# Squared-ReLU attention and a mixture-of-depths FFN on one core: score and index operations moved to VectorE, the sigmoid issued later, a load split around the FFN weights

## The chip, the core and the metric

The kernel runs on one core of a Trainium2 chip. The metric is the time of one execution in microseconds on the device; lower is better. In the text PE is TensorE, DVE is VectorE, ACT is ScalarE and POOL is GpSimd. Each engine executes its own queue of instructions in order and waits at an instruction until its inputs and its output buffer are ready.

## What is computed

For 8 batches of 12 heads, 448 tokens and 64 elements per head, attention without a softmax, and on its result, seen as 448 rows of 768, a feed-forward layer (FFN) for the 128 rows of each batch with the highest score:

```python
scores = scale * np.matmul(q, k.transpose(0, 1, 3, 2))
attn = np.maximum(scores, 0.0) ** 2 / S
x = np.matmul(attn, v)                  # then heads side by side: (8, 448, 768)
...
scores = np.einsum('bsd,d->bs', x, w_gate)
out = x.copy()
for b in range(B):
    top_idx = np.argpartition(-scores[b], capacity)[:capacity]
    xe = x[b, top_idx]
    h = np.maximum(xe @ w1, 0.0)
    ye = h @ w2
    g = 1.0 / (1.0 + np.exp(-scores[b, top_idx]))
    out[b, top_idx] = x[b, top_idx] + g[:, None] * ye
```

The FFN is 768 to 1024 to 768, and the inputs are float32; the kernel works in bfloat16.

## The kernel before

**Attention in pairs.** The work is cut into 48 steps t, one for each pair of heads, six to a batch (L356). `transposes(t)` (L152) turns q and k of a pair with PE and copies them out of PSUM on DVE (qkt, L170). `scores(t, c)` (L173) computes one of four chunks of keys; `relu_square` (L187) applies Relu on ACT (r_sb, L192) and squares on DVE (a_sb, L193); `attend` (L196) multiplies by v and, after the last chunk, ACT copies the result to xT (L210). Step t issues the scores of chunks 0 and 1, the attend of chunks 2 and 3 of step t-1, the transposes of step t+1, then the scores of chunks 2 and 3 and the attend of chunks 0 and 1.

**The MoE of a batch** is the generator `moe(b)` (L216). It becomes active when the batch's attention is done, and `advance` (L341) issues a piece of it twice in each step of the next batch, by a credit in microseconds; the `yield` numbers are the pieces' prices. So the MoE of batch b runs among the six pairs of batch b+1, and that of batch 7 by itself at the end. It computes the scores of all tokens (sc_ps, L221), copies them (bc, L224), transposes x chunk by chunk into x_sb (L230, L233), turns the scores into columns (cols, L242), splits each score into three bfloat16 parts that are written to columns 2 to 4 of tok (L245 to L250; columns 0 and 1 hold the row number as two integers), counts each token's rank on DVE with a tie-break table (L257), and makes from the rank a one-hot matrix (hot, L273). A matmul of hot and tok gives the row number and score of each of the 128 chosen tokens (sel_ps, L280), and DVE copies it (sel, L283). From sel come the row index idx (L286, L287), the score g (L289, L290) and its sigmoid on ACT (L291). hot also gathers the rows (xe_ps, L300); two layers follow (h_ps, L311; ye_ps, L323); ACT scales by g (gye, L327), and an indirect DMA adds the result to the output rows (L330), which were stored before by L269.

**Queues.** Every DMA is issued by POOL, in program order: `load(b, h0, h1)` (L96) makes nine DMAs, one for q, four for k and four for v. In order POOL issues the load of batch 0 in three parts with the identity matrix between, the gate weights, w1 and w2 (L117, L118), the load of batch 1 (L119), three kinds of tables by iota (slot_i L128, tie_i L134, tok_i L141 and L142), and then what belongs to the steps: the load of batch b+2 at the first step of batch b (L370), and the POOL work of moe. DVE turns the tables into slot_row (L130), tie (L136) and tok (L146); these are ahead of the loop in the program, and the framework chooses where they stand in DVE's queue. Inside the loop the order of the instructions on each engine is that of the program. There are three buffers each of q, k and v, and two of x_sb and of tok.

Of the kernel before, what the change touches and what calls it, by code (L numbers as in the profile page):

```python
# [8 lines left out]
FP32 = mybir.dt.float32  # L9
# [3 lines left out]
AF = mybir.ActivationFunctionType  # L13
ALU = mybir.AluOpType
# [6 lines left out]
def kernel(  # L21
# [11 lines left out]
    nc = tc.nc  # L33

    B, H, S, Dh = q.shape
    HD = H * Dh
    F = moe_w1.shape[1]
    CAP = int(moe_capacity)
    P = 112
    NC = S // P  # L40
# [14 lines left out]
    small = ctx.enter_context(tc.tile_pool(name="small", bufs=2))  # L55
# [23 lines left out]
    def load_q(b, h0, h1):  # L79
        nc.gpsimd.dma_start(  # L80
            out=q_sb[b % NBUF][:, h0:h1],
            in_=q[b, h0:h1].rearrange("h (p c) d -> p h c d", c=NC))

    def load_kv(t_sb, src, b, h0, h1):
        t = t_sb[b % NBUF]
        for par in range(2):
            hs = slice(h0 + par, h1, 2)
            lo, hi = (4, 3) if par == 0 else (3, 4)
            nc.gpsimd.dma_start(  # L89
                out=t[0:64, hs, 0:lo, :],  # L90
                in_=src[b, hs, 0:64 * lo].rearrange("h (p c) d -> p h c d", c=lo))
            nc.gpsimd.dma_start(  # L92
                out=t[64:128, hs, 0:hi, :],
                in_=src[b, hs, 64 * lo:S].rearrange("h (p c) d -> p h c d", c=hi))

    def load(b, h0, h1):  # L96
        load_q(b, h0, h1)
        load_kv(k_sb, k, b, h0, h1)
        load_kv(v_sb, v, b, h0, h1)
# [10 lines left out]
    for i in range(1, NBUF):  # L110
        zero_halves(i)

    wg_cols = const.tile([128, NM], BF16)
    nc.gpsimd.dma_start(out=wg_cols, in_=moe_w_gate.rearrange("(m p) -> p m", p=128))
    w1_sb = const.tile([128, NM, F], BF16)
    w2_sb = const.tile([128, NF, HD], BF16)
    nc.gpsimd.dma_start(out=w1_sb, in_=moe_w1.rearrange("(m p) f -> p m f", p=128))  # L117
    nc.gpsimd.dma_start(out=w2_sb, in_=moe_w2.rearrange("(m p) f -> p m f", p=128))  # L118
    load(1, 0, H)  # L119

    wg_rep = const.tile([128, NM, 128], BF16)
    nc.vector.tensor_copy(out=wg_rep,
                          in_=wg_cols.unsqueeze(2).to_broadcast([128, NM, 128]))
# [13 lines left out]
                            op0=ALU.is_gt, op1=ALU.mult)  # L137
# [78 lines left out]
    def moe(b):  # L216
# [21 lines left out]
        for c in range(NC):  # L238
            nc.tensor.matmul(out=col_ps[:, c:c + 1], lhsT=bc[0:1, c * P:(c + 1) * P],
                             rhs=one_f, is_transpose=True, start=(c == 0), stop=(c == NC - 1))  # L240
        cols = small.tile([P, NC], FP32, name="cols")
        nc.vector.tensor_copy(out=cols, in_=col_ps)  # L242
        tk = tok[b % 2]
        rem = small.tile([P, NC, 2], FP32, name="rem")
        nc.gpsimd.tensor_copy(out=tk[:, :, 2], in_=cols)  # L245
        nc.gpsimd.tensor_tensor(out=rem[:, :, 0], in0=cols, in1=tk[:, :, 2], op=ALU.subtract)
        nc.gpsimd.tensor_copy(out=tk[:, :, 3], in_=rem[:, :, 0])
        nc.gpsimd.tensor_tensor(out=rem[:, :, 1], in0=rem[:, :, 0], in1=tk[:, :, 3],
                                op=ALU.subtract)
        nc.gpsimd.tensor_copy(out=tk[:, :, 4], in_=rem[:, :, 1])  # L250
        yield 0.3

        rank = small.tile([P, NC], FP32, name="rank")
# [2 lines left out]
        def rank_chunk(c):  # L256
# [17 lines left out]
            out=hot, in0=slot_row.unsqueeze(1).to_broadcast([P, NC, CAP]),  # L274
            in1=rank.unsqueeze(2).to_broadcast([P, NC, CAP]), op=ALU.is_equal)
# [6 lines left out]
        sel = small.tile([CAP, 5], FP32, name="sel")  # L282
        nc.vector.tensor_copy(out=sel, in_=sel_ps)  # L283
        idx = small.tile([CAP, 1], INT32, name="idx")
        row = small.tile([CAP, 1], FP32, name="row")
        nc.gpsimd.tensor_tensor(out=row, in0=sel[:, 0:1], in1=sel[:, 1:2], op=ALU.add)  # L286
        nc.gpsimd.tensor_copy(out=idx, in_=row)  # L287
        g = small.tile([CAP, 1], FP32, name="g")
        nc.gpsimd.tensor_tensor(out=g, in0=sel[:, 4:5], in1=sel[:, 3:4], op=ALU.add)  # L289
        nc.gpsimd.tensor_tensor(out=g, in0=g, in1=sel[:, 2:3], op=ALU.add)  # L290
        nc.scalar.activation(out=g, in_=g, func=AF.Sigmoid)  # L291
        yield 0.2

        xeT = moe_pool.tile([128, NM, CAP], BF16, name="xeT")
# [11 lines left out]
        for half in range(2):  # L306
# [8 lines left out]
            nc.scalar.activation(out=hT[:, half * 4:half * 4 + 4, :], in_=ps, func=AF.Relu)  # L315
            yield 0.67

        gye = moe_pool.tile([CAP, HD], FP32, name="gye")
        for half in range(2):
            cols_d = slice(half * 384, half * 384 + 384)  # L320
# [10 lines left out]
            out=out.rearrange("b s d -> (b s) d"),  # L331
            out_offset=bass.IndirectOffsetOnAxis(ap=idx[:, :1], axis=0),
            in_=gye, in_offset=None, element_offset=b * S * HD, compute_op=ALU.add)
# [19 lines left out]
    with tc_manual:  # L353
        transposes(0)
        share = MOE_US / (2 * NHP) * 1.05
        for t in range(NT + 1):  # L356
            b, hp = divmod(t, NHP)
            if t < NT:
                scores(t, 0)
                scores(t, 1)  # L360
                relu_square(t, 0)
                relu_square(t, 1)
            if t > 0:
                attend(t - 1, 2)
                attend(t - 1, 3)
                if t % NHP == 0:
                    active.append(moe(t // NHP - 1))
            if t < NT:
                if hp == 0 and b + 2 < B:
                    load(b + 2, 0, H)  # L370
                if t + 1 < NT:
                    transposes(t + 1)
                advance(share)
                scores(t, 2)
                scores(t, 3)
                relu_square(t, 2)
                relu_square(t, 3)
                attend(t, 0)
                attend(t, 1)
                advance(share)  # L380
        while active:
            advance(10.0)
# [35 lines left out]
```

## Time and profile before

| | us |
|---|---|
| median of 3 runs | 312.34 |
| lowest and highest run | 312.20, 314.26 |
| the profiled execution | 315.93 |
| its span, first to last instruction | 314.2 |
| PE busy | 238.0 (76%) |
| ACT busy | 196.6 (63%) |
| DVE busy | 176.6 (56%) |
| POOL busy | 103.8 (33%) |

The rows further down come from one profiled execution. Times in them are microseconds from the start of its span. A line of a timeline names the start, the duration, the engine, the line of the kernel, the operation, the tile written and the tiles read, shapes, how many instructions are merged, and in brackets how long the engine stood idle before and what ended that wait. A digit of the busy tenths covers 1/40 of the span, 7.9 us.

### The profile page before, as it was taken

The numbers are of one execution on the slowest core, as the hardware profiler recorded it, in microseconds if no ns is written. First come the engines' busy times: TensorE is split into PE (matmuls) and PEld (weight loads), VectorE is DVE, ScalarE is ACT, GpSimd is POOL, SyncE is SP. The second block draws the span as 40 slices with busy tenths as digits, with TensorE's granted clock in tenths as the row PEclk, the third lists the DMA queues.
The fourth block names the chain that finished last, engine by engine and source line by source line (L and its number), as shares of the span: only waits on it lengthen the run. The fifth ranks groups of instructions, "written<-read, shape, count | busy, mean of one in ns | idle before, by whom it ended". The sixth has DMA issues, their size and how long they took to land.

```text
span 314.2 us, 6208 instructions
## 1 busy us (share of the span) xinstructions
PE 238.0 (76%) x2496; PEld 134.4 (43%) x2496; DVE 176.6 (56%) x378; ACT 196.6 (63%) x306; POOL 103.8 (33%) x191
## 2 busy tenths in 40 slices
PE   2597029649985899759984999499979998799480
PEld 1143014426452554436443554255445545455460
DVE  4378006934668165954577466936595568664500
ACT  1399006646974489728882799459875887496120
POOL 8991065730091204550085007420221023102301
PEclk9999756968997799979999899979995999799785
DMA  3999999993079801990099505990214012401603
GB/s 42 112 156 211 206 193 172 192 224 129 2 92 180 218 2 15 173 272 34 2 120 189 184 0 70 184 241 0 32 22 176 2 7 46 175 2 11 217 0 50
DMA packets 41580, 34.21 MB, mean 109 GB/s; under 512 B 14800, under 2 KB 38864, under 8 KB 40656
## 3 DMA queue, kind: packets, MB, share of 16 engines
q0 software_dynamic: 41552, 33.83, 64.2%
q8 instruction: 19, 0.31, 0.4%
q14 instruction: 9, 0.07, 0.1%
HBM read 39.32 MB, written 14.16 MB: 170 GB/s over the span
## 4 chain that ended last, share of the span: by engine, by line
PE 28%; issue 24%; DMA 24%; POOL 11%; DVE 6%; ACT 4%; POOLq 1%; ACTq 0%; DVEq 0%
DMA q_sb<-in_q_dram 13%; DMA k_sb<-in_k_dram 7%; PE o_ps L204 7%; PE s_ps L180 5%; PE h_ps L311 4%; PE ye_ps L323 4%; DMA out_dram<-x_sb 3%; ACT r_sb L192 3%; DVE trash L257 2%; PE xe_ps L300 2%; POOL v_sb L92 2%; PE s_ps L184 2%; DVE x_sb L233 2%; POOL tok L245 2%; POOL k_sb L89 1%
## 5 line engine op out<-in xcount | busy, mean ns | idle before, releaser
L192 ACT ACTIVATE r_sb<-s_ps 128x896 bf16<-128x896 f32 x192 | 148.2, 829 | 50.7 <-PE s_ps L180 49.5
L193 DVE TENSOR_TENSOR a_sb<-r_sb 128x896 bf16<-128x896 bf16 x192 | 103.6, 563 | 86.6 <-ACT r_sb L192 86.2
L204 PE MATMUL o_ps<-a_sb,v_sb 128*64 128x448 bf16 x384 | 61.6, 397 | 2.0 <-DVE a_sb L193 1.7
L330 POOL DMA_INDIRECT out_dram<-gye,idx x8 | 13.4, 1674 | 130.7 <-ACT gye L327 130.7
L180 PE MATMUL s_ps<-qkt 64*128 64x448 bf16 x288 | 50.0, 383 | 2.2 <-ACT r_sb L192 1.0
L170 DVE COPY qkt<-t_ps 128x960 bf16<-128x960 bf16 x48 | 31.2, 650 | 20.2 <-PE t_ps L165 20.2
L159 PE MATMUL t_ps<-ident,q_sb 112*64 112x112 bf16 x384 | 19.4, 224 | 20.0 <-DMA q_sb<-in_q_dram 14.5
L204 PEld LDWEIGHTS <-v_sb 128*64 128x64 bf16 x384 | 18.6, 112 | 32.1 <-issue 26.3
L311 PE MATMUL h_ps<-xeT,w_sb 128*128 128x128 bf16 x384 | 28.1, 227 | 1.3 <-ACT xeT L302 1.3
L159 PEld LDWEIGHTS <-q_sb 112*64 112x64 bf16 x384 | 17.6, 118 | 26.3 <-DMA q_sb<-in_q_dram 20.1
L92 POOL DMA_DIRECT2D v_sb<-in_v_dram x20 | 16.5, 824 | 36.8 <-DMA q_sb<-in_q_dram 21.3
L210 ACT ACTIVATE xT_sb<-o_ps 128x448 bf16<-128x448 f32 x48 | 26.6, 554 | 0.0
L311 PEld LDWEIGHTS <-w_sb 128*128 128x128 bf16 x384 | 23.6, 102 | 5.5 <-issue 4.3
L291 ACT ACTIVATE g<-g 128x1 f32<-128x1 f32 x8 | 1.6, 203 | 38.6 <-POOL g L290 38.6
L323 PE MATMUL ye_ps<-w_sb,hT 128*128 128x384 bf16 x128 | 24.9, 328 | 0.0
L180 PEld LDWEIGHTS <-qkt 64*128 64x128 bf16 x288 | 12.8, 95 | 28.4 <-issue 20.4
L165 PE MATMUL t_ps<-ident,k_sb 128*64 128x128 bf16 x384 | 21.4, 229 | 3.8 <-DMA k_sb<-in_k_dram 3.8
L230 PE MATMUL x_ps<-ident,xT_sb 128*112 128x128 bf16 x192 | 15.8, 223 | 10.0 <-DVE x_sb L233 8.0
L257 DVE SCALAR_TENSOR_TENSOR trash<-bc,cols,tie 112x448 bf16<-112x448 f32 x32 | 21.6, 675 | 0.2
L89 POOL DMA_DIRECT2D v_sb<-in_v_dram x20 | 19.1, 958 | 7.0 <-DMA w_sb<-in_moe_w_dram 6.8
L280 PE MATMUL sel_ps<-tok,hot 112*128 112x5 bf16 x32 | 2.0, 168 | 25.5 <-POOL tok L250 18.5
L300 PE MATMUL xe_ps<-hot,x_sb 112*128 112x128 bf16 x192 | 20.1, 284 | 0.0
(57 smaller groups left out, 250.4 us busy)
## 6 DMA issues: line engine op xcount, KB each, us to landing
out_dram<-x_sb POOLq DMA_DIRECT2D x8, 1344.0 KB, 6.2
q_sb<-in_q_dram POOLq DMA_DIRECT2D x7, 672.0 KB, 10.1
w_sb<-in_moe_w_dram POOLq DMA_DIRECT2D x2, 1536.0 KB, 16.0
k_sb<-in_k_dram POOLq DMA_DIRECT2D x14, 192.0 KB, 10.3
v_sb<-in_v_dram POOLq DMA_DIRECT2D x14, 192.0 KB, 8.0
k_sb<-in_k_dram POOLq DMA_DIRECT2D x14, 144.0 KB, 10.2
v_sb<-in_v_dram POOLq DMA_DIRECT2D x14, 144.0 KB, 11.0
q_sb<-in_q_dram POOLq DMA_DIRECT2D x1, 336.0 KB, 5.1
```

Source lines behind the costliest of these rows:

```text
L92: nc.gpsimd.dma_start(out=t[64:128, hs, 0:hi, :], in_=src[b, hs, 64 * lo:S].rearrange("h (p c) d -> p h c d", c=hi))
L159: nc.tensor.matmul(out=ps[64 * hh:64 * hh + 64, c * P:(c + 1) * P], lhsT=qs[:, h0 + hh, c, :], rhs=ident[:P, :P], is_transpose=True, start ...
L170: nc.vector.tensor_copy(out=sb, in_=ps)
L180: nc.tensor.matmul(out=ps[:, hh, :S], lhsT=sb[rows, S + c * 128:S + (c + 1) * 128], rhs=sb[rows, :S], start=True, stop=True)
L192: nc.scalar.activation(out=r[:, :n], in_=ps[:, :n, :S], func=AF.Relu)
L193: nc.vector.tensor_tensor(out=a[:, :n], in0=r[:, :n], in1=r[:, :n], op=ALU.mult)
L204: nc.tensor.matmul(out=o_ps[t][rows, :], lhsT=vs[:, 2 * hp + hh, c, :], rhs=a[:, hh if c < 3 else 0, :], start=(c == 0), stop=(c == 3), sk ...
L210: nc.scalar.activation(out=xT[b][:, hp, :], in_=o_ps.pop(t), func=AF.Copy, scale=o_scale)
L257: nc.vector.scalar_tensor_tensor(out=trash, in0=bc[:P, :], scalar=cols[:, c:c + 1], in1=tie[:, c, :], op0=ALU.subtract, op1=ALU.is_ge, acc ...
L300: nc.tensor.matmul(out=ps[:, mm, :], lhsT=x_sb[:, c, m * 128:(m + 1) * 128], rhs=hot[:, c, :], start=(c == 0), stop=(c == NC - 1))
L311: nc.tensor.matmul(out=ps[:, ff, :], lhsT=w1_sb[:, m, f * 128:(f + 1) * 128], rhs=xeT[:, m, :], start=(m == 0), stop=(m == NM - 1))
L323: nc.tensor.matmul(out=ps, lhsT=hT[:, f, :], rhs=w2_sb[:, f, cols_d], start=(f == 0), stop=(f == NF - 1))
```

## The change

Four edits. The five POOL operations that split the score become four on DVE (the last subtraction writes its result into tok directly), and rem has half its size. The two POOL operations for idx become one addition on DVE that writes an integer, and the two for g become one on DVE. The sigmoid is issued behind the first FFN layer, ahead of gye. The load of batch 1 is issued in two parts: heads 0 to 3 ahead of the FFN weights, heads 4 to 11 behind them, eighteen DMAs in place of nine.

```diff
     wg_cols = const.tile([128, NM], BF16)
     nc.gpsimd.dma_start(out=wg_cols, in_=moe_w_gate.rearrange("(m p) -> p m", p=128))
+    load(1, 0, 4)
     w1_sb = const.tile([128, NM, F], BF16)
     w2_sb = const.tile([128, NF, HD], BF16)
     nc.gpsimd.dma_start(out=w1_sb, in_=moe_w1.rearrange("(m p) f -> p m f", p=128))
     nc.gpsimd.dma_start(out=w2_sb, in_=moe_w2.rearrange("(m p) f -> p m f", p=128))
-    load(1, 0, H)
+    load(1, 4, H)
...
         tk = tok[b % 2]
-        rem = small.tile([P, NC, 2], FP32, name="rem")
-        nc.gpsimd.tensor_copy(out=tk[:, :, 2], in_=cols)
-        nc.gpsimd.tensor_tensor(out=rem[:, :, 0], in0=cols, in1=tk[:, :, 2], op=ALU.subtract)
-        nc.gpsimd.tensor_copy(out=tk[:, :, 3], in_=rem[:, :, 0])
-        nc.gpsimd.tensor_tensor(out=rem[:, :, 1], in0=rem[:, :, 0], in1=tk[:, :, 3],
-                                op=ALU.subtract)
-        nc.gpsimd.tensor_copy(out=tk[:, :, 4], in_=rem[:, :, 1])
+        rem = small.tile([P, NC], FP32, name="rem")
+        nc.vector.tensor_copy(out=tk[:, :, 2], in_=cols)
+        nc.vector.tensor_tensor(out=rem, in0=cols, in1=tk[:, :, 2], op=ALU.subtract)
+        nc.vector.tensor_copy(out=tk[:, :, 3], in_=rem)
+        nc.vector.tensor_tensor(out=tk[:, :, 4], in0=rem, in1=tk[:, :, 3], op=ALU.subtract)
         yield 0.3
...
         idx = small.tile([CAP, 1], INT32, name="idx")
-        row = small.tile([CAP, 1], FP32, name="row")
-        nc.gpsimd.tensor_tensor(out=row, in0=sel[:, 0:1], in1=sel[:, 1:2], op=ALU.add)
-        nc.gpsimd.tensor_copy(out=idx, in_=row)
+        nc.vector.tensor_tensor(out=idx, in0=sel[:, 0:1], in1=sel[:, 1:2], op=ALU.add)
         g = small.tile([CAP, 1], FP32, name="g")
-        nc.gpsimd.tensor_tensor(out=g, in0=sel[:, 4:5], in1=sel[:, 3:4], op=ALU.add)
-        nc.gpsimd.tensor_tensor(out=g, in0=g, in1=sel[:, 2:3], op=ALU.add)
-        nc.scalar.activation(out=g, in_=g, func=AF.Sigmoid)
+        nc.vector.scalar_tensor_tensor(out=g, in0=sel[:, 4:5], scalar=sel[:, 3:4],
+                                       in1=sel[:, 2:3], op0=ALU.add, op1=ALU.add)
         yield 0.2
...
+        nc.scalar.activation(out=g, in_=g, func=AF.Sigmoid)
         gye = moe_pool.tile([CAP, HD], FP32, name="gye")
```

## Rows read from the trace of the kernel before

**Rows 1.** The page, busy tenths of 40 slices: PE and the DMA engines.
```profile
PE   2597029649985899759984999499979998799480
...
DMA  3999999993079801990099505990214012401603
```

**Rows 2.** List of waits: engine, line, waited for; us in total, times, longest.
```profile
ACT g L291 <- POOL g L290: 38.6, 8, 7.0
...
PE sel_ps L280 <- POOL tok L250: 18.5, 5, 4.1
```

**Rows 3.** Timeline of PE where the load of batch 1 lands.
```profile
42.70 0.58 PE L159 MATMUL t_ps<-ident,q_sb 112*64 112x112 bf16 x8 [12.05 <-DMA q_sb<-in_q_dram]
...
46.39 0.60 PE L165 MATMUL t_ps<-ident,k_sb 128*64 128x128 bf16 x7 [1.58 <-DMA k_sb<-in_k_dram]
```

**Rows 4.** Timeline of POOL: w1, the last v of batch 1, tie_i.
```profile
19.02 0.84 POOL L117 DMA_DIRECT2D w_sb<-in_moe_w_dram  x1
...
42.94 0.66 POOL L92 DMA_DIRECT2D v_sb<-in_v_dram  x1 [2.83 <-DMA q_sb<-in_q_dram]
...
43.80 1.65 POOL L134 IOTA tie_i<- 112x1792 int32 x1
```

**Rows 5.** DMA issues: queue, count, KB each, median us to landing.
```profile
q_sb<-in_q_dram POOLq DMA_DIRECT2D x7, 672.0 KB, 10.1
...
v_sb<-in_v_dram POOLq DMA_DIRECT2D x2, 24.0 KB, 2.1
```

**Rows 6.** Timeline of DVE in batch 1, pairs 6 and 7.
```profile
52.38 1.08 DVE L136 TENSOR_SCALAR tie<-tie_i 112x1792 f32<-112x1792 int32 x1
...
54.30 0.93 DVE L193 TENSOR_TENSOR a_sb<-r_sb 128x896 bf16<-128x896 bf16 x2 [0.68 <-ACT r_sb L192]
...
57.39 0.65 DVE L170 COPY qkt<-t_ps 128x960 bf16<-128x960 bf16 x1
...
62.73 0.69 DVE L273 TENSOR_TENSOR hot<-slot_row,rank 112x512 bf16<-112x512 f32 x1
```

**Rows 7.** Timeline of PE: sel_ps of moe 0, 1, 2, 5; xe_ps of moe 2, 5, 6.
```profile
67.01 0.25 PE L280 MATMUL sel_ps<-tok,hot 112*128 112x5 bf16 x4 [4.07 <-POOL tok L250]
...
102.91 0.24 PE L280 MATMUL sel_ps<-tok,hot 112*128 112x5 bf16 x4 [3.04 <-POOL tok L250]
...
137.22 0.25 PE L280 MATMUL sel_ps<-tok,hot 112*128 112x5 bf16 x4 [3.80 <-POOL tok L250]
137.33 1.44 PE L300 MATMUL xe_ps<-hot,x_sb 112*128 112x128 bf16 x12
...
236.38 0.27 PE L280 MATMUL sel_ps<-tok,hot 112*128 112x5 bf16 x4 [1.60 <-DVE hot L273]
236.51 1.44 PE L300 MATMUL xe_ps<-hot,x_sb 112*128 112x128 bf16 x12
...
269.30 0.83 PE L300 MATMUL xe_ps<-hot,x_sb 112*128 112x128 bf16 x12
```

**Rows 8.** Timeline of POOL ahead of sel_ps of moe 2.
```profile
134.03 0.66 POOL L92 DMA_DIRECT2D v_sb<-in_v_dram  x1 [4.38 <-DMA q_sb<-in_q_dram]
134.68 1.40 POOL L245 CAST tok<-cols 112x4 bf16<-112x4 f32 x1
```

**Rows 9.** Timeline of DVE: hot of moe 1 and 2, cols and first rank of moe 5.
```profile
98.91 0.69 DVE L273 TENSOR_TENSOR hot<-slot_row,rank 112x512 bf16<-112x512 f32 x1
...
134.27 0.69 DVE L273 TENSOR_TENSOR hot<-slot_row,rank 112x512 bf16<-112x512 f32 x1
...
230.65 0.15 DVE L242 COPY cols<-col_ps 112x4 f32<-112x4 f32 x1
230.84 0.69 DVE L257 SCALAR_TENSOR_TENSOR trash<-bc,cols,tie 112x448 bf16<-112x448 f32 x1
```

**Rows 10.** Timeline of ACT in batch 1: the table load, the idle after hT.
```profile
63.55 1.28 ACT L291 ACT_TABLE_LOAD   x1
...
80.42 1.35 ACT L192 ACTIVATE r_sb<-s_ps 128x896 bf16<-128x896 f32 x2 [0.34 <-PE s_ps L180]
```

## The prediction

> **What bounds the kernel now.** I read the page first. PE's busy tenths are near 9 over most of the span, with two kinds of holes: a deep one, of two slices, where the DMA row is full, and a shallow one once in every batch [rows 1]. So TensorE (PE) sets the end wherever it is fed, and the question is what starves it. The list of waits answers for the shallow holes: PE waited five times, 18.5 us in all, for the GpSimd (POOL) instruction that writes the last column of tok, and ScalarE (ACT) stood 38.6 us before the sigmoid, for POOL's g [rows 2].
>
> The timelines give the places. I call the MoE of batch b "moe b"; it runs among the pairs of batch b+1, and pair 6 is the first of batch 1. The deep hole: PE stands 12.05 us until the q of batch 1 lands at 42.70 and is not free of k before 46.39 [rows 3]. On POOL's queue the weights stand ahead of that load: w1 is issued at 19.02, and the last v of batch 1 only at 42.94, after a wait for q; the iota tables come behind it, tie_i until 45.45 [rows 4]. The shallow holes: sel_ps of moe 0, 1 and 2 starts after 4.07, 3.04 and 3.80 us of idle PE; moe 3 and 4 repeat moe 2 (4.07 + 3.04 + 3 x 3.80 = 18.5). In moe 5 the wait is 1.60 us and VectorE's (DVE's) hot ends it [rows 7]. Why POOL is late is in its queue: in moe 2 it stands 4.38 us in front of the last v load of a batch needed much later, issues it at 134.03, and only then does the cast of L245 run, in 1.40 us [rows 8].
>
> **The split load.** It removes nothing from the transfers; it puts a third of batch 1 (heads 0 to 3, pairs 6 and 7) before the weights. A load is 672 KB each of q, k and v [rows 5]. At the rate of k behind q, 672 KB in 46.39 - 42.70 = 3.7 us, that is 182 KB/us [rows 3, 5]. Pairs 6 and 7 then need 672 KB issued by POOL from 19.02 in nine DMAs; one issue takes about 0.66 us [rows 4], so all are out by about 25 and landed before PE asks for them (at 42.70 - 12.05 = 30.65 [rows 3]). The hole moves to pair 8, whose q and k are now behind the weights. When they land, 224 KB more (the v of heads 0 to 3) has gone through than at 46.39: 1.2 us. Also the DMA engines may run short while POOL issues nine small DMAs: 9 x 0.66 = 5.9 us of issue for 672/182 = 3.7 us of data, so between 0 and 2.2 us lost; I take 1.0, as earlier loads still drain at first. Pair 8's k lands at 46.4 + 1.2 + 1.0 = 48.6 (47.6 to 49.8).
>
> What is late next is the tables. The last v issue now waits for the q of heads 4 to 11, which lands 448/182 = 2.5 us before that k, at 46.1. From the last v issue to the end of tie_i took 45.45 - 42.94 = 2.5 us [rows 4], so 48.6 again; DVE's tie takes 1.08 us, to 49.7 [rows 6]. Behind tie and tok on DVE stand, by the program, the four new operations of moe 0 (0.72 us, below), two squares of pair 7 (0.93) and then pair 8's qkt [rows 6]: qkt starts at 49.7 + 0.7 + 0.9 = 51.4, where the transposes alone would allow 49.2. From the start of that qkt to the end of hot is 63.42 - 57.39 = 6.03 us in the trace [rows 6]; I keep that, so hot ends at 57.4 and sel_ps of moe 0 starts at 57.5 in place of 67.01 [rows 7]: 9.5 us gained, POOL's wait of 4.07 included. By the bounds of the landing alone it is 8.3 to 10.5; without tables in the way, 2.2 more. Behind the nine new issues on POOL the load of batch 2 and the store of batch 0 come later too, by no more than the tables do; batch 2 is wanted six pairs after the hole and the store only before moe 0's scatter, so I price that at nothing (if that cover failed, at the same 2 to 3 us).
>
> Here the Trainium skill speaks against the change. "DMA: Bandwidth & Descriptors", section "Anatomy of one DMA", gives every GpSimd DMA a fixed time of some 2.0 us beside its bytes. Nine more DMAs would by it, if nothing overlapped, be an estimated 18 us in front of the weights; that is a rival below, worked out from rows. The trace's issues 0.66 us apart speak for overlap.
>
> **The score splits on DVE.** Five POOL operations become four on DVE, between cols and the first rank. DVE doing them is not in the trace. The nearest row is a small operation followed by one that depends on it: cols at 230.65, rank at 230.84, 0.19 us from start to start [rows 9]. Four at about 0.18 are 0.72 us a batch. At the least it is nothing (a DVE wait for ACT that stands behind them absorbs them), at the most 4 x 0.69 = 2.8 us were each as long as that rank [rows 9]; the 0.18 is by far the nearest. What stands behind them is two squares, the ranks, three x copies and hot, so sel is later by what isn't absorbed.
>
> With POOL out of the chain, sel_ps starts at the later of two: PE's arrival (start less idle [rows 7]) and the end of hot.
> - moe 1: PE arrives at 102.91 - 3.04 = 99.87, hot ended at 99.60 [rows 7, 9]; with up to 0.72 more, sel starts near 100.2: 2.7 gained. The lower clock that follows the 3 us of idle costs something too: twelve xe matmuls took 1.44 us behind the stall of moe 2 against 0.83 at the full clock [rows 7], and the low stretch held some two and a half times as much work as those, about 1.4 us. I count 0.5 of it here: 3.2.
> - moe 2, 3, 4: PE arrives at 133.42, hot ends at 134.96 [rows 7, 9] and would end at about 135.5, sel 0.1 later: 137.22 - 135.6 = 1.6, of which I keep 1.5, as PE still idles over 2 us and the clock still falls: 4.5 for the three.
> - moe 5, 6, 7: hot already was the last to come. Nothing is removed and 0.7 is added to each: -2.1.
>
> **idx, g and the sigmoid.** Four POOL operations become two on DVE behind sel's copy, where DVE waits for ACT anyway; nobody but the scatter, far later, needs them: nothing (up to 0.4 us a batch if a square were ready). ACT no longer stands before the sigmoid, but in the full stretches PE is the slower, so this alone I put at nothing. One price: the table load of 1.28 us ran at 63.55, within ACT's wait [rows 10]; now it comes with the sigmoid of moe 0, before gye, where ACT's idle is 0.34 us [rows 10]. Between 0 and 1.3 us, once; I take 0.6.
>
> **Sum.** 9.5 - 0.6 + 3.2 + 4.5 - 2.1 = 14.5 us. The profiled execution took 315.93 us (span 314.2 and 1.7 around it), 1.1% above the median 312.34; it would come to 301.4. The holes are those of every execution, so I take the same microseconds from the median: 312.34 - 14.5 = 297.8.
>
> **Rivals.**
> - *The tables hold pair 6.* If slot_row, tie and tok stand in DVE's queue ahead of the squares of pair 6, these wait to about 49.7, and pair 6 is where it was. Then sel of moe 0 gains only 67.01 - (63.42 + 0.8) = 2.8, and the whole is 297.8 + 6.7 = 304.5. For it: in the trace tie ran just there, at 52.38 [rows 6]. Against: there it came late and held nothing up, and nine more issues ahead of the iotas put it later still. 0.12.
> - *The clock eats the batches.* A stall of 1.60 us in moe 5 was followed by slow xe as well [rows 7]; if a shorter stall is followed by as much again at the low clock, moe 1 to 4 give back 4 x 1.4 = 5.6: 303.4. 0.12.
> - *Better.* The tables hold nothing (2.2) and two batches keep their clock (2.8): 292.8. 0.14.
> - *Slower: the nine DMAs run one after another.* Place: between load 0 and w1. Price: the smallest load took 2.1 us to land [rows 5], nine in a row 18.9; pair 8's k lands at 46.4 + 1.2 + 18.9 = 66.5, 17.9 later than I have it: 315.7. Slower begins once that k lands after 48.6 + 14.5 = 63.1. Against: loads of batch 0 were issued in the same way and landed together. That is the rule of the skill, without overlap. 0.04, of which 0.02 in a half-way form near no change.
>
> My forecast has 0.58. The range reaches from the better case to the first rival, 292.5 to 304.5; it takes in the bounds of landing, tables, table load and splits. A difference under 1% a measurement of this kernel can hardly tell from none. All cases but the last are 2.5 to 6% faster: faster 0.95, same 0.03, slower 0.02.
>
> **What would show it.** In the profile after: PE's hole begins near 39 instead of 31 and ends for pair 8 at 48 to 50; tie on DVE ends near 49.7; sel of moe 0 near 57.5. No PE wait for POOL's tok; sel waits for hot, about 0.3 us in moe 1, 2.2 in moe 2 to 4, 2.3 in moe 5; four small DVE operations 0.2 us apart after each cols. ACT's table load next to the sigmoid. Wrong would be k of pair 8 after 52, squares of pair 6 after 49, or batches as long as before although the POOL wait is gone.

## The result, and the profile after

The changed kernel takes 294.49 us (median; 293.26 to 297.19), the kernel before 312.73 beside it: a ratio of 0.942, 95% interval 0.935 to 0.950, 18.2 us less. The prediction was 297.8, range 292.5 to 304.5. The profiled execution took 294.19 us with a span of 291.8. A ratio below is not always the quotient of the medians: where the executions of a kernel lie apart, it can go by the faster of them.

The clock line of the page before, then the page after, busy tenths and granted clock in 40 slices (7.3 us each now):

```profile
PEclk9999756968997799979999899979995999799785
```
```profile
PE   1598924799959997899978998699869995997570
PEclk9999995699998999579986999999999999999595
DMA  3999999999599709950399009950322030403504
```

The hole, slices of 0 and 2 in [rows 1], has become slices of 2 and 4. The clock is low at the hole (5 and 6), a little in moe 1 (8), in moe 2 (5 and 7), in moe 3 (8 and 6) and at the end; from moe 4 to the last batch the line is full, which it was not before. The timeline of PE after, at the hole (the first line is the last work ahead of it):

```profile
38.07 0.57 PE L205 MATMUL o_ps<-a_sb,v_sb 128*64 128x448 bf16 x4
46.41 0.59 PE L160 MATMUL t_ps<-ident,q_sb 112*64 112x112 bf16 x8 [7.78 <-DMA q_sb<-in_q_dram]
...
48.92 0.61 PE L166 MATMUL t_ps<-ident,k_sb 128*64 128x128 bf16 x7 [0.93 <-DMA k_sb<-in_k_dram]
...
52.63 0.80 PE L231 MATMUL x_ps<-ident,xT_sb 128*112 128x128 bf16 x6 [1.64 <-DVE x_sb L234]
...
57.22 0.26 PE L279 MATMUL sel_ps<-tok,hot 112*128 112x5 bf16 x4
```

These answer to [rows 3] and the first of [rows 7]: the wait for q is 7.78 us instead of 12.05, it comes two pairs later, PE has k at 48.92, and sel_ps of moe 0 starts at 57.22 with no wait in front, where it was 67.01. POOL's timeline after, for [rows 4]:

```profile
25.35 0.86 POOL L118 DMA_DIRECT2D w_sb<-in_moe_w_dram  x1
...
46.65 0.61 POOL L92 DMA_DIRECT2D v_sb<-in_v_dram  x1 [1.71 <-DMA q_sb<-in_q_dram]
...
47.47 1.65 POOL L135 IOTA tie_i<- 112x1792 int32 x1
```

w1 is issued 6.3 us later, yet the last v and the tables are only 3.7 us later. DVE after, in moe 0 (compare [rows 6] and [rows 9]):

```profile
38.70 0.18 DVE L246 CAST tok<-cols 112x4 bf16<-112x4 f32 x1
38.92 0.16 DVE L247 TENSOR_TENSOR rem<-cols,tok 112x4 f32<-112x4 f32 x1
...
49.56 0.66 DVE L171 COPY qkt<-t_ps 128x960 bf16<-128x960 bf16 x1 [9.01 <-PE t_ps L166]
...
50.27 1.09 DVE L137 TENSOR_SCALAR tie<-tie_i 112x1792 f32<-112x1792 int32 x1
...
51.42 0.68 DVE L256 SCALAR_TENSOR_TENSOR trash<-bc,cols,tie 112x448 bf16<-112x448 f32 x1
...
56.47 0.69 DVE L272 TENSOR_TENSOR hot<-slot_row,rank 112x512 bf16<-112x512 f32 x1
```

The new operations follow each other by 0.2 us and run before the hole; the tables stand between qkt of pair 8 and the first rank of moe 0. The list of waits, for [rows 2], has no wait for POOL's tok any more; what is late at sel_ps is hot, and ACT's stand is now for the xe matmuls themselves:

```profile
ACT xeT L298 <- PE xe_ps L296: 24.3, 11, 7.7
...
PE sel_ps L279 <- DVE hot L272: 10.5, 6, 3.0
```

Last, the table load of [rows 10], on ACT's timeline, and beside it the PE instruction that waits for the Relus behind it:

```profile
68.32 1.28 ACT L314 ACT_TABLE_LOAD   x1
69.61 0.20 ACT L314 ACTIVATE g<-g 128x1 f32<-128x1 f32 x1
69.72 1.33 ACT L193 ACTIVATE r_sb<-s_ps 128x896 bf16<-128x896 f32 x2
...
```
```profile
70.67 0.80 PE L181 MATMUL s_ps<-qkt 64*128 64x448 bf16 x4 [0.52 <-ACT r_sb L193]
```

Cutting both spans at the same places of PE's timeline shows where the 22.4 us between the two profiled executions lie. A stage "moe n" runs from the first sc_ps matmul of moe n to that of moe n+1. The clock is the mean granted clock of the stage, as a share of 2.4 GHz.

| stage | before, us | after, us | gain | forecast | clock before | clock after |
|---|---|---|---|---|---|---|
| start to sel_ps of moe 0 | 67.01 | 57.22 | 9.8 | 9.5 | 0.86 | 0.88 |
| sel_ps of moe 0 to moe 1 | 20.34 | 19.16 | 1.2 | -0.6 | 0.87 | 1.00 |
| moe 1 | 35.35 | 31.92 | 3.4 | 3.2 | 0.90 | 0.95 |
| moe 2 | 34.24 | 33.75 | 0.5 | 1.5 | 0.95 | 0.85 |
| moe 3 | 33.63 | 32.05 | 1.6 | 1.5 | 0.95 | 0.89 |
| moe 4 | 33.59 | 30.66 | 2.9 | 1.5 | 0.95 | 1.00 |
| moe 5 | 32.82 | 30.64 | 2.2 | -0.7 | 0.90 | 1.00 |
| moe 6 | 30.47 | 29.56 | 0.9 | -0.7 | 0.94 | 1.00 |
| moe 7 to the end | 26.8 | 26.8 | -0.1 | -0.7 | 0.75 | 0.74 |

The medians differ by 18.2, less than these 22.4: the profiled execution before was 3 us above its median. The terms to explain are moe 4 to 6, of which the forecast had moe 5 and 6 as small losses. Moe 5 before and after (its sel_ps and xe_ps before are in [rows 7]):

```profile
224.16 1.12 PE L221 MATMUL sc_ps<-xT_sb,wg_rep 128*128 128x448 bf16 x5
...
256.98 1.12 PE L221 MATMUL sc_ps<-xT_sb,wg_rep 128*128 128x448 bf16 x5
```
```profile
204.76 1.12 PE L222 MATMUL sc_ps<-xT_sb,wg_rep 128*128 128x448 bf16 x5
...
217.66 0.26 PE L279 MATMUL sel_ps<-tok,hot 112*128 112x5 bf16 x4 [1.60 <-DVE hot L272]
217.78 0.83 PE L296 MATMUL xe_ps<-hot,x_sb 112*128 112x128 bf16 x12
...
235.40 1.12 PE L222 MATMUL sc_ps<-xT_sb,wg_rep 128*128 128x448 bf16 x5
```

Up to sel_ps the batch is 0.7 us longer than before (12.90 for 12.22), as forecast; behind sel_ps it is 2.9 us shorter (17.74 for 20.60), and the xe matmuls run at the full clock, where they ran at half before.

### The profile page after: what moved, and what is told of

Same layout as the page of the kernel before. It is cut to its first block, busy times and chain, and to the rows that moved or that the text cites. A ratio compares the mean times of both kernels' runs of the same rounds, so it can differ in the third digit from the quotient of the medians.

```text
span 291.8 us, 6198 instructions
## 1 busy us (share of the span) xinstructions
PE 231.8 (79%) x2496; PEld 132.2 (45%) x2496; DVE 184.4 (63%) x426; ACT 196.8 (67%) x306; POOL 88.8 (30%) x128
## 4 chain that ended last, share of the span: by engine, by line
PE 46%; DVE 19%; DMA 10%; ACT 9%; POOL 8%; issue 5%; POOLq 1%; ACTq 0%
PE o_ps L205 10%; PE s_ps L181 9%; PE h_ps L307 7%; ACT r_sb L193 7%; DMA k_sb<-in_k_dram 7%; PE ye_ps L320 7%; DVE trash L256 5%; DVE a_sb L194 4%; PE xe_ps L296 4%; DVE x_sb L234 4%; PE s_ps L185 3%; DMA q_sb<-in_q_dram 2%; PE t_ps L166 2%; DMA out_dram<-x_sb 2%; POOL k_sb L89 2%
## 5 line engine op out<-in xcount | busy, mean ns | idle before, releaser
L205 PE MATMUL o_ps<-a_sb,v_sb 128*64 128x448 bf16 x384 | 59.5, 384 | 3.0 <-DVE a_sb L194 2.6
L181 PE MATMUL s_ps<-qkt 64*128 64x448 bf16 x288 | 49.2, 376 | 2.7 <-ACT r_sb L193 1.3
L205 PEld LDWEIGHTS <-v_sb 128*64 128x64 bf16 x384 | 19.2, 110 | 33.0 <-issue 27.5
L92 POOL DMA_DIRECT2D v_sb<-in_v_dram x22 | 17.5, 796 | 31.8 <-DMA q_sb<-in_q_dram 12.5
L231 PE MATMUL x_ps<-ident,xT_sb 128*112 128x128 bf16 x192 | 16.7, 231 | 12.6 <-DVE x_sb L234 10.6
L298 ACT CAST xeT<-xe_ps 128x384 bf16<-128x384 f32 x16 | 7.6, 478 | 25.0 <-PE xe_ps L296 24.3
L89 POOL DMA_DIRECT2D v_sb<-in_v_dram x22 | 20.1, 921 | 8.6 <-DMA w_sb<-in_moe_w_dram 7.2
L231 PEld LDWEIGHTS <-xT_sb 128*112 128x112 bf16 x192 | 13.8, 137 | 17.6 <-issue 17.1
L89 POOL DMA_DIRECT2D k_sb<-in_k_dram x22 | 20.9, 954 | 0.0
```

The costliest lines, as they stand in the source:

```text
L89: nc.gpsimd.dma_start(out=t[0:64, hs, 0:lo, :], in_=src[b, hs, 0:64 * lo].rearrange("h (p c) d -> p h c d", c=lo))
L181: nc.tensor.matmul(out=ps[:, hh, :S], lhsT=sb[rows, S + c * 128:S + (c + 1) * 128], rhs=sb[rows, :S], start=True, stop=True)
L205: nc.tensor.matmul(out=o_ps[t][rows, :], lhsT=vs[:, 2 * hp + hh, c, :], rhs=a[:, hh if c < 3 else 0, :], start=(c == 0), stop=(c == 3), sk ...
L231: nc.tensor.matmul(out=x_ps[:, m * 128:(m + 1) * 128], lhsT=xTb[:, m, c * P:(c + 1) * P], rhs=ident, is_transpose=True, start=(m == 0), st ...
```

## The experiments

**1 and 2: the parts apart.** First the split alone on the kernel before:

```diff
+    load(1, 0, 4)
     w1_sb = const.tile([128, NM, F], BF16)
...
-    load(1, 0, H)
+    load(1, 4, H)
```

> The kernel before with the split load alone. Theory (the two parts need each other): moe 0's columns of tok are written by POOL behind the load of batch 3, whose last v issue ended at 68.8 us in the changed kernel; with about 1.2 us of POOL operations sel_ps of moe 0 starts near 70, three later than the 67.01 of before, although pairs 6 and 7 run early; the rest as before: about 315, ratio 1.00 to 1.01. Rival (the parts add): the split is worth its 9 us alone: about 304, ratio 0.97.

Measured: 316.81 us, ratio 1.012 (1.006 to 1.018): the load that was to help makes this kernel slower. PE reaches sel_ps of moe 0 at 57.89 and stands there; its line, and POOL's in the same run:

```profile
69.62 0.25 PE L281 MATMUL sel_ps<-tok,hot 112*128 112x5 bf16 x4 [11.73 <-POOL tok L251]
```
```profile
67.61 0.66 POOL L92 DMA_DIRECT2D v_sb<-in_v_dram  x1 [3.06 <-DMA q_sb<-in_q_dram]
68.26 0.21 POOL L246 CAST tok<-cols 112x4 bf16<-112x4 f32 x1
```

and POOL's in the kernel before:

```profile
65.66 0.21 POOL L245 CAST tok<-cols 112x4 bf16<-112x4 f32 x1
```

What the pairs gained in front, PE lost behind POOL, whose queue the nine extra DMAs had made longer: the cast of moe 0 stands in both behind the last v issue of batch 3, and comes 2.6 us later. The rival that the parts add is out.

Then everything but the split:

```diff
-    load(1, 0, 4)
...
-    load(1, 4, H)
+    load(1, 0, H)
```

> The changed kernel with the load of batch 1 in one piece behind the weights. By the prediction's terms only moe 0's 4.07 us wait shrinks to about 1.2 at the start and the batches give 3.2 + 4.5 - 2.1: about 305. If what moe 4 to 6 gained in the changed kernel (2.9, 2.2 and 0.9 us of stage) comes from the code and not from the phase of the clock, the batches give 11.5 us again and it is 298. sel_ps of moe 0 near 64.2 in both.

Measured: median 299.15 us (294.64 to 300.37), ratio 0.955 (0.949 to 0.961), between the two numbers expected. Its profiled execution is its fastest; there moe 1 to 6 take 31.48, 31.25, 30.59, 30.68, 30.65 and 29.56 us, with a granted clock of 1.00 from moe 3 to 6; sel_ps of moe 0 starts at 62.30 (64.2 expected). So 30.6 us in the middle batches is what this code takes at the full clock. The other three executions take 3 to 6 us more, at a mean clock of 0.913 to 0.920 against 0.936; why they lost it was open.

**3: the sigmoid back at its place.** ACT stood 38.6 us before it in the kernel before [rows 2], and I had priced its move at nothing.

```diff
         nc.vector.scalar_tensor_tensor(out=g, in0=sel[:, 4:5], scalar=sel[:, 3:4],
                                        in1=sel[:, 2:3], op0=ALU.add, op1=ALU.add)
+        nc.scalar.activation(out=g, in_=g, func=AF.Sigmoid)
         yield 0.2
...
-        nc.scalar.activation(out=g, in_=g, func=AF.Sigmoid)
         gye = moe_pool.tile([CAP, HD], FP32, name="gye")
```

> The changed kernel with the sigmoid at its old place ahead of xe. Theory (the sigmoid's place is worth nothing): ACT waits for g, now from DVE behind two squares and a qkt, about 1 us a batch, mostly while PE works; the table load is covered again, 0.5 us back: 294 to 296, ratio to the kernel before 0.94 to 0.947. Rival (ACT's wait for g was what held moe 4 to 6 of the kernel before): these stages go back to 33.6, 32.8 and 30.5 us, 300, ratio 0.96.

Measured: 297.62 us (297.00 to 298.61), ratio 0.949 (0.945 to 0.953), beyond the theory's 296 and short of the rival's 300. In moe 4, 5 and 6 the stages are 32.10, 31.64 and 31.07; stretches of low clock lie in the first and the last, while moe 5 is 1.0 us longer than in the changed kernel (30.64) with both at the full clock. That points to the sigmoid, in one batch of one execution.

**4: the clock.** In the changed kernel moe 2 and moe 4 show how the clock can make such a difference. Two pairs of lines from PE's timeline after:

```profile
121.16 0.27 PE L279 MATMUL sel_ps<-tok,hot 112*128 112x5 bf16 x4 [0.95 <-DVE hot L272]
121.29 1.44 PE L296 MATMUL xe_ps<-hot,x_sb 112*128 112x128 bf16 x12
...
187.02 0.26 PE L279 MATMUL sel_ps<-tok,hot 112*128 112x5 bf16 x4 [1.60 <-DVE hot L272]
187.14 0.83 PE L296 MATMUL xe_ps<-hot,x_sb 112*128 112x128 bf16 x12
```

The shorter wait is followed by matmuls at half clock (1.2 GHz; granted clock 0.50 from 121.2 to 122.7), the longer one by matmuls at the full 2.4 GHz (1.00 from 187.1 to 188.0): a stall of this size sometimes costs the clock and sometimes not. So I filled it, with five matmuls into unused columns of the sel_ps bank, which nobody reads:

```diff
-        sel_ps = m_ps_pool.tile([CAP, 5], FP32, name="sel_ps", tag="m")
+        sel_t = m_ps_pool.tile([CAP, 512], FP32, name="sel_ps", tag="m")
+        sel_ps = sel_t[:, 0:5]
+        for _ in range(5 if b >= 2 else 0):
+            nc.tensor.matmul(out=sel_t[:, 64:512], lhsT=ident, rhs=xTb[:, 0, :],
+                             start=True, stop=True, skip_group_check=True)
```

> The changed kernel with five matmuls of 448 columns, whose result nobody reads, ahead of sel_ps in moe 2 to 7 (about 0.95 us at the full clock, in a stall of 0.95 to 3 us). Theory (the idle of PE there costs again through the clock that falls behind it): fewer stretches at half clock, stages of moe 2 and 3 of 31 instead of 33.75 and 32.05: 291 to 293. Rival (the clock has nothing to do with these stalls): 294.5 to 295.5, with as many low stretches.

Measured: 291.24 us, ratio 0.929 (0.925 to 0.932), and six runs within 290.40 to 291.83, where the changed kernel spread over 293.3 to 297.2. Stages of moe 2 and 3: 31.55 and 30.59 instead of 33.75 and 32.05. The granted clock on this run's page, against the line of the page after:

```profile
PEclk9999995599997999799999999999999999999595
```

One mark below 9 is left in moe 2 and none from there to the last batch. The filler of moe 4 in the trace:

```profile
182.05 1.12 PE L280 MATMUL sel_ps<-xT_sb,ident 128*128 128x448 bf16 x5
```

More work in the same place makes the kernel faster and its times alike. Moe 4 to 6, which had the full clock without it, take the same time with it (30.67, 30.64 and 29.57 us for 30.66, 30.64 and 29.56), so the matmuls themselves cost nothing there, and these stalls cost mostly through the clock. The filler does not always keep the clock up: in experiment 7 moe 3, with filler, took 31.44 us at 0.95. It still gives a base on which the rest can be measured.

**5 and 6: sigmoid and idx, g on that base.** The edit of experiment 3 on the kernel with filler:

> The kernel with filler (291.2 us) and the sigmoid at its old place. Theory, formed after the first four runs (ACT's stand before the sigmoid delays the xe copy and the Relus behind it by 1.0 us in every batch that also feeds pairs): with the clock kept up, the stages of moe 3 to 6 become 1.0 us longer (31.6 for 30.6, 30.6 for 29.6), moe 1 and 2 as well, the table load gives 0.5 back: 296 to 298. Rival (the longer stages of that run were the clock's): 290.5 to 292.

Measured: 295.20 us (294.06 to 296.50), ratio 0.943 (0.938 to 0.948): 4.0 us. moe 3 to 6 take 31.60, 31.69, 31.64 and 30.57 instead of 30.59, 30.67, 30.64 and 29.57, which is 1.0 each; the sum came out below the 5 to 7 expected, since moe 1 did not change, moe 2 lost 0.6, and moe 7 to the end came out 0.8 shorter. In moe 4, with the sigmoid early, ACT and then PE:

```profile
187.35 0.20 ACT L292 ACTIVATE g<-g 128x1 f32<-128x1 f32 x1 [3.33 <-DVE g L290]
187.46 0.46 ACT L303 CAST xeT<-xe_ps 128x384 bf16<-128x384 f32 x1
187.82 1.36 ACT L193 ACTIVATE r_sb<-s_ps 128x896 bf16<-128x896 f32 x2
```
```profile
185.34 0.26 PE L283 MATMUL sel_ps<-tok,hot 112*128 112x5 bf16 x4 [0.55 <-DVE hot L272]
...
188.79 0.80 PE L181 MATMUL s_ps<-qkt 64*128 64x448 bf16 x4 [0.64 <-ACT r_sb L193]
```

and with the sigmoid late, the same instructions:

```profile
184.70 0.48 ACT L302 CAST xeT<-xe_ps 128x384 bf16<-128x384 f32 x1 [2.30 <-PE xe_ps L300]
185.08 1.36 ACT L193 ACTIVATE r_sb<-s_ps 128x896 bf16<-128x896 f32 x2
```
```profile
183.72 0.26 PE L283 MATMUL sel_ps<-tok,hot 112*128 112x5 bf16 x4 [0.55 <-DVE hot L272]
...
186.47 0.55 PE L181 MATMUL s_ps<-qkt 64*128 64x448 bf16 x4
```

g comes from DVE behind two squares and a qkt; with the sigmoid early:

```profile
185.20 1.15 DVE L194 TENSOR_TENSOR a_sb<-r_sb 128x896 bf16<-128x896 bf16 x2
186.27 0.65 DVE L171 COPY qkt<-t_ps 128x960 bf16<-128x960 bf16 x1
...
187.10 0.21 DVE L290 SCALAR_TENSOR_TENSOR g<-sel 128x1 f32<-128x1 f32 x1
```

ACT stands for it with the Relus of the next scores in its queue: they start 2.5 us after sel_ps instead of 1.4, and PE, which has two score buffers, waits for one of them. PE's four score matmuls start 3.45 us after sel_ps instead of 2.75 and take 0.80 us instead of 0.55, which makes the 1.0 us. No run has the sigmoid early and g from POOL, as in the kernel before, at the full clock; so what its wait cost there is known only by this neighbour.

idx and g back on POOL, the sigmoid late:

```diff
+        row = small.tile([CAP, 1], FP32, name="row")
+        nc.gpsimd.tensor_tensor(out=row, in0=sel[:, 0:1], in1=sel[:, 1:2], op=ALU.add)
+        nc.gpsimd.tensor_copy(out=idx, in_=row)
-        nc.vector.tensor_tensor(out=idx, in0=sel[:, 0:1], in1=sel[:, 1:2], op=ALU.add)
...
+        nc.gpsimd.tensor_tensor(out=g, in0=sel[:, 4:5], in1=sel[:, 3:4], op=ALU.add)
+        nc.gpsimd.tensor_tensor(out=g, in0=g, in1=sel[:, 2:3], op=ALU.add)
-        nc.vector.scalar_tensor_tensor(out=g, in0=sel[:, 4:5], scalar=sel[:, 3:4],
-                                       in1=sel[:, 2:3], op0=ALU.add, op1=ALU.add)
```

> The kernel with filler and idx and g made on POOL as before, the sigmoid late. Theory (with the sigmoid late nobody on the path waits for g): only moe 0 loses about 1 us, since POOL comes to g at about 70.5, behind the load of batch 3, and the sigmoid stands until then; later batches unchanged: 291 to 292.5. Rival (g on DVE matters in every batch): 0.5 us or more in each, 294 and above.

Measured: median 293.40 us (288.55 to 294.46), ratio 0.927 (0.919 to 0.935). The time is inconclusive: the interval covers the ratio of the kernel with filler, 0.929, and the median lies between the two forecasts. The profiled execution says more: its hole ended 2.2 us late, sc_ps of moe 0 already 2 us late, before any of the edited lines run, and from moe 4 on its stages are 30.74, 30.64 and 29.56, the same as on DVE at the same full clock. In moe 0 the sigmoid waited 0.44 us for POOL, for the 1 us expected. So the theory's second half holds in these stages, and the total stays open by a microsecond or two.

**7 and 8: the two big parts on that base.** The split load taken out again, as in experiment 2:

> The kernel with filler, the load of batch 1 in one piece behind the weights. Theory (with POOL out of the chain the split is worth what its own stage shows: the first sc_ps of moe 1 at 76.7 with it, at 81.5 in the run without it, 4.8 us): 296, later stages as with the split, 30.6 to 31.6. Rival (the split's 9 us of the sum): 300.

Measured: 295.34 us (294.64 to 296.92), ratio 0.942 (0.939 to 0.946). The split is worth 4.1 us here, near the theory's 4.8. And the score split back on POOL, the five old operations for the four new:

> The kernel with filler, with only the score split back on POOL (idx and g on DVE, sigmoid late, load split). Theory (the split of the scores is what POOL's queue holds): sel_ps of moe 0 near 70 instead of 57.5, POOL waits of 2 to 4 us in moe 1 to 4, less 0.7 us of DVE work in each: about 291 + 12 + 4 x 1.5 = 309, not far from the kernel before though three of its four edits are in. Rival (the sigmoid and idx, g carry the gain): 297 or less.

Measured: 311.94 us (309.61 to 312.98), ratio 0.995 (0.992 to 0.998), 3 us above the theory's 309. Split load, idx and g on DVE, late sigmoid and filler together are worth 0.5% while POOL makes tok. Its list of waits (compare [rows 2]):

```profile
PE sel_ps L285 <- POOL tok L251: 21.2, 5, 11.5
```

Its moe 5 and 6, where POOL has no loads ahead, take 29.96 and 28.87 us against 30.64 and 29.57 with DVE: there the move costs the 0.7 that was predicted.

**9 and 10: further.** The hole that is left waits for the rest of batch 1 behind w1 and w2, and those are first used by moe 0. So the whole load goes ahead:

```diff
-    load(1, 0, 4)
+    load(1, 0, H)
...
-    load(1, 4, H)
```

> The changed kernel with the whole load of batch 1 ahead of the weights. Theory (what the hole of 8 us waits for is a load behind 3 MB of weights that nobody needs before the first layer of moe 0): no hole at pair 8, tables early, sel_ps of moe 0 near 48 instead of 57.2, w1 landed by 43 and w2 by 51 before their first use; the load of batch 2 lands near 61, just ahead of pair 12: 285 to 288. Rival (the queue of transfers is the bound, the hole only moves to the weights or to pair 12): 291 or more.

Measured: 282.61 us, ratio 0.899 (0.894 to 0.905), better than expected. PE in this run:

```profile
31.46 0.41 PE L165 MATMUL t_ps<-ident,k_sb 128*64 128x128 bf16 x7 [0.61 <-DMA k_sb<-in_k_dram]
...
43.94 0.80 PE L230 MATMUL x_ps<-ident,xT_sb 128*112 128x128 bf16 x6 [3.67 <-DVE x_sb L233]
...
49.08 0.27 PE L278 MATMUL sel_ps<-tok,hot 112*128 112x5 bf16 x4
```

0.6 us of waiting for k is all that is left of the hole; the longest wait there is now for DVE's x copies, 3.67 us, and sel_ps of moe 0 starts at 49.08.

With it the filler and a sigmoid on one element ahead of the loop, whose table load then runs at 0.74 us, with ACT idle:

> The whole load of batch 1 ahead of the weights, the filler, and a sigmoid on one element at the start so that its table is loaded before anything waits for ACT. Theory (the three terms add: 9, 3 and 0.5 us): 281 to 284, no ACT table load in batch 1, stages of moe 1 to 6 of 30.6 to 31.5. Rival (one of them hides another): 286 or more.

Measured: 279.27 us (277.00 to 280.29), ratio 0.890 (0.885 to 0.895). It beats the changed kernel by 15 us. Both numbers are below the expected ones by 2: the gains add, and the hole had cost clock too (mean granted clock up to sel_ps of moe 0: 0.88 in the changed kernel, 0.94 and 0.96 in these two).

## Why the prediction was right

The mechanism held, the time came out 3.3 us under the forecast and inside the range, and one step was wrong. Part of the closeness is luck, as said below.

- **The split load.** k of pair 8 at 48.92 (forecast 48.6), sel_ps of moe 0 at 57.22 (57.5). The inside of this step was off: the four operations of tok did not wait for the tables, they ran at 38.70, and qkt of pair 8 was not held until 51.4 but began at 49.56. The tables held the first rank instead, for 1.3 us, and PE, at half clock from 46.4 to 55, waited 1.64 us for an x copy behind that rank. hot ended at 57.16 all the same (57.4), so two errors of inner order offset each other: that this term came out within 0.3 us is luck in part. Experiment 9 shows the rest: without the hole 12 us are to be had.
- **The fixed time per DMA.** The Trainium skill, "DMA: Bandwidth & Descriptors", section "Anatomy of one DMA", gives each DMA a fixed time of some 2.0 us, for the nine an estimated 18 us if they ran one after another. The trace shows that they did not: w1 was issued 6.3 us later, and PE had k of pair 8 only 48.92 - 46.39 = 2.5 us after the old time for k. The slower rival is out, but experiment 1 shows a slower way that I had not listed: the same nine issues ahead of POOL's tok.
- **The score splits.** Right where it can be read apart, from a batch's first sc_ps to its sel_ps: 2.2, 1.7, 1.7 and 1.5 us shorter in moe 1 to 4 (forecast 2.7, then 1.5 each), 0.7, 0.7 and 0.6 longer in moe 5 to 7 (0.7 each); experiment 8 gives the same 0.7. The waits that were to remain at sel_ps are shorter than forecast (0.95, 0.95 and 1.60 us in moe 2 to 4 for 2.2), because PE itself came later (in moe 2 11.9 us after the first sc_ps for 10.7), which the forecast had left out. What the sum did not say is that this edit is the one on which the others rest: 20.7 us with the others in place (311.94 - 291.24).
- **The step that failed:** "ACT no longer stands before the sigmoid, but in the full stretches PE is the slower, so this alone I put at nothing." PE is the slower on average, but the sigmoid stood ahead of Relus that PE's next scores need, with two score buffers between them. Measured 1.0 us in each of moe 3 to 6 (experiment 5), 4.0 in all. The medians gained 3.7 us more than forecast (18.2 - 14.5), the profiled executions 7.9, and nearly all of that lies behind sel_ps, where the sigmoid stood: there the batches gained 7.6 us and the forecast had -0.1. The sigmoid is about half of it. The other half goes with the clock: moe 4 to 6 had 0.90 to 0.95 before and 1.00 after, and moe 2 and 3 lost some of theirs. So moe 5 gained 2.2 us where a loss was predicted by both; that split is an estimate from the stages, no run makes it. The wait list had shown the sigmoid: 38.6 us on ACT [rows 2], and a long wait on an engine with other work in its queue is not free because the engine is idle elsewhere.
- **The table load**: 0.52 us of waiting on PE, forecast 0.6. No run took it out alone.
- **The clock rival** came true in single batches only: moe 2 at 33.75 and moe 3 at 32.05, with a granted clock of 0.85 and 0.89. Moe 4 to 6 kept their clock in this execution. That is in part luck: a stall of the same 1.60 us was followed by half clock in moe 5 before and in moe 4 of experiment 3. The Trainium skill says in "TensorE: Matmul & The Clock Gate", section "What's actually happening", that the low state is the default and activity lifts it. The trace agrees: the filler's 1.1 us of otherwise useless matmuls in a batch brought 3.2 us (294.49 - 291.24) and the spread of runs from 1.3% (four) to 0.5% (six). What decides which stall loses the clock was not tried.

## What to carry to other kernels

An in-order queue that issues transfers is no place for small operations on the path: they come when the queue's transfers allow it, and an earlier or longer transfer makes them later. Price a wait by what stands behind it on its own engine, and by how many buffers the consumer has left, not by the engine's busy share. When a part that ought to help shows nothing, look for the queue that gives it back before dropping it: here one edit alone made the kernel 1.2% slower and was worth 4 us once the other was in.

## What was not expected of the hardware

A cast of four elements a partition on DVE took 0.18 us in moe 0, and 0.68 and 0.47 in moe 1, while POOL was issuing the load of batch 4:

```profile
81.03 0.68 DVE L246 CAST tok<-cols 112x4 bf16<-112x4 f32 x1
...
81.93 0.47 DVE L248 CAST tok<-rem 112x4 bf16<-112x4 f32 x1
```

The subtractions beside them kept their 0.16 and 0.17. In moe 2 and 3 the two casts took 0.28 and 0.42, in moe 5 to 7, where POOL has no load to issue, 0.17 to 0.18. The other way round it was in [rows 8], where POOL's cast took 1.40 us beside DVE's squares; that the two engines hold each other up is an inference from these rows, no run was made for it. And an unneeded matmul can pay: five of them in a stall made the kernel 1.1% faster.
